# Loading w_in in four transfers of 128 partitions, with v read by even and odd columns

## The chip, the cores and the metric

The kernel runs on one core of a Trainium2 chip. The metric is the device time of one execution in microseconds (us). The core has a matrix engine (PE, whose weight loads are listed apart as PEld), a vector engine (DVE), a scalar engine (ACT), GpSimd (POOL) and a queue engine (SP); transfers run on 16 DMA engines.

## What is computed

Causal attention with 16 extra "beacon" keys in front that every query sees, and behind it a two-layer network with ELU between the layers. The heads of the attention, side by side, are the rows that the network takes.

```python
# q, k, v: (B=8, H=8, S=576, D=64); beacon_k, beacon_v: (8, 8, 16, 64)
k_all = np.concatenate([beacon_k, k], axis=2)
v_all = np.concatenate([beacon_v, v], axis=2)
scores = scale * np.matmul(q, k_all.transpose(0, 1, 3, 2))
scores = np.where(causal, -1000000000.0, scores)
a = softmax(scores)
x = np.matmul(a, v_all).transpose(0, 2, 1, 3).reshape(B * S, H * D)   # (4608, 512)
h = x @ w_in                                   # w_in (512, 2048)
g = np.where(h > 0.0, h, np.exp(np.minimum(h, 0.0)) - 1.0)
out = g @ w_out                                # w_out (2048, 512)
```

## The kernel before

Attention goes batch by batch (b = 0 to 7), the network by tiles of 512 tokens (tile 0 and 1 of 256 each, so that the network can begin early). The program is one list of steps in a string (from line 824 on). Each word names a step and its numbers, and the steps' instructions go to their engines in the order of that list; nothing reorders them. Each engine works through its own instructions in that order, and a wait of one instruction holds up all that stand behind it on its engine.

The steps that matter here:

- `lq.b.n.h0.h1` loads q and k of batch b (segment n, heads h0 to h1), `lv.b.j` a block j of 128 keys of v (with j = 0 also the beacon rows), `wi` a part of w_in, `wo.i` a quarter of w_out. All of these are transfers issued by POOL, which also turn fp32 into 16-bit numbers on the way. `s` and `J` store results through SP's queue.
- `T` transposes q and k on PE, `ck` and `cq` copy the result out of PSUM, `S` multiplies keys and queries, `x` takes the exponential on ACT, `m` masks on DVE.
- `L` sums the exponentials with a weight of ones on PE, `n` makes the reciprocal on ACT, `W` multiplies with v on PE, and `M` scales the product on DVE and writes it to xT, the network's input with features on the partitions. `W` and `L` use `quad` (line 381): four heads at a time, each in 32 columns of the PE array. A head has 64 columns of v, so it takes two such products, called halves. Half t of heads 4g to 4g+3 becomes chunk 2g + t of xT.
- `F.t.i` multiplies xT by two (tiles 0 and 1) or one (later tiles) column blocks of w_in, each over 4 chunks. `e`, `u`, `r`, `k`, `g` make the ELU, `G` and `Q` multiply with w_out.
- `wm` and `wh` multiply zeros on PE; their results aren't used.

w_in lies in SBUF as 128 partitions x 4 chunks x 2048 columns. The order of its rows follows from the halves: before, half t takes columns 32t to 32t+31 of a head, so partition 32i + d of chunk 2g + t is row 256g + 64i + 32t + d of w_in. One transfer, `wi.c.n` (line 158), brings 32 partitions (i) of two chunks (g) and one half of the columns (c): 32 x 2 pieces of 4 KB, 128 KB once in 16 bits. Sixteen of them load the whole. `F.0.0` to `F.0.3` and `F.1.0` to `F.1.3` use the lower half of the columns (c = 0), the next blocks the upper.

In the list two of the sixteen stand ahead of `lv.0.2`, the last block of v that `W.0.A` needs; six more of the lower half stand ahead of `F.0.1`, and the eight of the upper half between `lv.0.4` and `wo.0`.

Of the kernel before, what the change touches and what calls it, by code (L numbers as in the profile page):

```python
# [17 lines left out]
def kernel(  # L18
# [11 lines left out]
    nc = tc.nc  # L30
    P = 128

    B, H, S, D = q.shape
# [4 lines left out]
    DF = moe_w_in.shape[1]  # L38
# [7 lines left out]
    kc = [min(P, SK - P * j) for j in range(NKC)]  # L46
# [53 lines left out]
    w_in16 = konst.tile([P, NCC, DF], FP16, name="w_in16")  # L100
# [51 lines left out]
                nc.gpsimd.dma_start(  # L152
                    out=vt[b][0:NB, 0, :, :], in_=beacon_v[b].rearrange("h n d -> n h d"))

    wi_v = moe_w_in.rearrange("(g i t d) f -> i d g t f", i=4, t=2, d=32)
    wo_v = moe_w_out.rearrange("(f p) m -> p f m", p=P)

    def load_wi(c, n):
        f_ = slice(DF // 2 * c, DF // 2 * (c + 1))
        g, i = n // 4, n % 4  # L160
        nc.gpsimd.dma_start(
            out=w_in16[32 * i:32 * (i + 1), 2 * g:2 * g + 2, f_], in_=wi_v[i, :, g, :, f_])

    def load_wo(i):
        nc.gpsimd.dma_start(out=w_out16[:, 4 * i:4 * (i + 1), :], in_=wo_v[:, 4 * i:4 * (i + 1), :])
# [3 lines left out]
    for b in range(B):  # L169
        (nc.sync if b % 2 == 0 else nc.scalar).dma_start(  # L170
            out=bk32[NB * b:NB * (b + 1), :, :],
            in_=beacon_k[b].rearrange("h n d -> n h d"))
    zero = lo[:, 2 * DM:3 * DM].bitcast(BF16)
    nc.vector.memset(zero, 0.0)
    ones = konst.tile([P, 32], FP16)
# [81 lines left out]
        load_qk(b, n_, h0, h1)  # L257

    @step
    def wi(c, n):  # L260
        load_wi(c, n)

    @step
    def T(b, p, n_):
# [39 lines left out]
    def et(b, p):  # L304
        if (b, p // 2) not in ets:
            ets[b, p // 2] = attn.tile([P, 2, EC2], FP16, tag="et", bufs=3, name="et")
        return ets[b, p // 2][:, :, ECOLS * (p % 2):ECOLS * (p % 2 + 1)]
# [73 lines left out]
    def quad(b, g, qa, qe, t, half, first):  # L381


        v16 = None if half is None else vt[b]
        pcs = [(j, max(a, qa), min(e, qe), c + max(a, qa) - a) for (j, a, e, c) in lays[b]
               if max(a, qa) < min(e, qe)]
        for n, (j, a, e, c) in enumerate(pcs):
            for i in range(4):
                h, p = 4 * g + i, 2 * g + i // 2
                nc.tensor.matmul(  # L390
                    out=t[32 * i:32 * (i + 1), a - qa:e - qa],
                    lhsT=ones[0:kc[j], :] if half is None else v16[0:kc[j], j, h, 32 * half:32 * (half + 1)],
                    rhs=et(b, p)[0:kc[j], i % 2, c:c + e - a],
                    start=(first and n == 0), stop=(n == len(pcs) - 1), skip_group_check=True)

# [21 lines left out]
    @step  # L417
    def L(b, g):


        if g == "A":
            t = bank("ops", name="la")
            for i in range(2):
                quad(b, i, 0, CUT, t[:, CUT * i:CUT * (i + 1)], None, i == 0)
            lt[b, g] = t
        elif g == "B":
            t = psum.tile([P, 2, 512], FP32, tag="S", name="lt")
            for i in range(2):
                quad(b, i, CUT, S, t[:, i, 0:S - CUT], None, True)
            lt[b, g] = t[:, :, 0:S - CUT]  # L430
        else:
            t = hd[b, g] = psum.tile([P, 1024], FP32, tag="S", name="lt")
            r_ = lt[b, g] = t[:, 512 - QA:512 - QA + S]
            if (b, g) in presum:
                for i in range(4):
                    nc.tensor.matmul(  # L436
                        out=r_[32 * i:32 * (i + 1), QA:S], lhsT=ones,
                        rhs=presum[b, g][:, i // 2, i % 2, QA:S], start=True, stop=True, skip_group_check=True)
            else:
                quad(b, g, QA, S, r_[:, QA:S], None, True)  # L440
            quad(b, g, 0, QA, r_[:, 0:QA], None, True)
            for half in range(2):
                quad(b, g, 0, QA, t[:, 512 - QA * (3 - half):512 - QA * (2 - half)], half, True)
# [383 lines left out]
    S.0.0.3 S.0.0.1 cb.1.0 x.0.0.3 lq.0.0.4.8 T.0.2.0 cq.0.2.0 T.0.3.0 x.0.0.1 S.0.1.2 x.0.1.2 wm.5  # L827
    S.0.1.1 x.0.1.1 wm.5 S.0.1.3 x.0.1.3 tri m.0.0.3 m.0.0.0 lq.0.1.4.8 T.0.2.1 cq.0.3.0 S.0.0.2
    x.0.0.2 wm.5 S.0.3.0 T.0.3.1 x.0.3.0 cq.0.2.1 lq.1.0.0.4 S.0.2.0 x.0.2.0 wm.5 S.0.2.1 x.0.2.1
    lv.0.0 lv.0.1 wm.5 S.0.2.3 x.0.2.3 wi.0.0 wi.0.7 lv.0.2 wm.4 T.1.1.0 ck.1.1.0 T.1.0.0 m.0.2.0  # L830
    m.0.1.0 m.0.3.0 L.0.A n.0.A m.0.1.2 m.0.0.2 cq.0.3.1 S.0.3.1 x.0.3.1 cq.1.0.0 W.0.A.0 M.0.A.0
    S.0.3.3 S.0.2.2 x.0.3.3 x.0.2.2 W.0.A.1 m.0.2.3 m.0.3.3 m.0.1.3 M.0.A.1 wh.3 S.0.3.2 wh.5 S.1.2
    x.0.3.2 x.1.2 wh.4 S.1.5 wi.0.5 wi.0.1 x.1.5 wi.0.3 wi.0.6 wi.0.2 wi.0.4 F.0.1 e.0.1 cb.1.1
    S.1.3 x.1.3 F.0.0 u.0.0 e.0.0 lv.0.4 wi.1.0 m.0.3.2 r.0.1 cb.1.2 m.0.2.2 L.0.B lv.0.3 wi.1.3
    W.0.B.0 n.0.B M.0.B.0 g.0.1 S.1.4 F.0.2 x.1.4 S.1.1 e.0.2 x.1.1 k.0.0 W.0.B.1 M.0.B.1 lq.1.0.4.8
    T.1.2.0 ck.1.2.0 r.0.2 g.0.2 F.1.1 u.1.1 e.1.1 T.1.3.0 cq.1.3.0 S.1.6 wi.1.1 cb.1.3 x.1.6 wi.1.7
    wi.1.6 wi.1.5 wi.1.2 wi.1.4 F.0.4 S.1.0 m.1.0.1 wo.0 e.0.4 r.0.4 g.0.4 x.1.0 F.1.7 e.1.7 k.1.1
    r.1.7 g.1.7 S.1.12 x.1.12 S.1.7 cb.2.2 G.0.0.0 x.1.7 F.0.5 e.0.5 r.0.5 S.1.9 x.1.9 g.0.5 F.0.7
    e.0.7 r.0.7 S.1.10 x.1.10 S.1.11 x.1.11 G.0.1.0 F.0.3 g.0.7 m.1.0.0 D.1.0.0 u.0.3 S.1.8 x.1.8
    e.0.3 m.1.1.0 D.1.1.0 k.0.3 F.1.6 u.1.6 cb.2.1 e.1.6 lq.2.0.0.8 T.2.3.0 ck.2.3.0 T.2.2.0  # L840
# [134 lines left out]
```

## Time and profile before

| | |
|---|---|
| median of 3 runs | 331.85 us (331.82 to 331.98) |
| the profiled execution | 332.93 us, of which the span of the profile is 331.2 us |
| granted clock of PE, mean | 0.994 |
| w_in | 16 transfers of 128 KB, median 6.7 us from issue to landing |
| v | 24 of 128 KB, 8 of 112 KB, 8 of 80 KB and 8 of 16 KB (beacons) |
| transfers issued by POOL | 94912 packets, 18.49 MB |

The span begins with the first instruction that the profile shows and ends with the last; times in the traces are us from its start. "Idle before" is time in which an engine waited, with what released it. Sizes of transfers are those that land, in 16 bits; w_in and w_out are read as fp32, twice as much. A line of a view by stretches has the stretch, its length, then busy us and, in brackets, the number of instructions of PE, PEld, DVE, ACT and POOL, then the granted clock of PE (1.00 is full), the DMA share and GB/s landed.

### The profile page before, as it was taken

To read this page: it belongs to the slowest core of one execution; us is meant where nothing else is said; L and a number is where in the kernel's file an instruction comes from. 1 tells how busy PE (TensorE), PEld (TensorE's weight loads), DVE (VectorE), ACT (ScalarE), POOL (GpSimd) and SP (SyncE) were. 2 spreads that over 40 slices of the span, in tenths; PEclk is the share of its full clock that TensorE was granted. 3 is DMA by queue.
4 is the path that set the end of the run, shared out by engine and by line. 5 is a ranking of instruction groups with operands and counts; after the bars stand their busy time and mean duration, and the time that the engine had idled before them with its cause. 6 is when DMAs were issued, how large, how long until landed. Compare 5 with 4: busy or idle time off the path is not lost.

```text
span 331.2 us, 8770 instructions
## 1 busy us (share of the span) xinstructions
PE 321.2 (97%) x3572; PEld 213.8 (65%) x3572; DVE 300.4 (91%) x568; ACT 291.8 (88%) x481; POOL 100.7 (30%) x121
## 2 busy tenths in 40 slices
PE   8989999999999979999999999999999999999995
PEld 3545666544445546765676566756766888888884
DVE  3573999999999799999999999999999999999981
ACT  1989999799999979999999999999988778889941
POOL 8866745583049218900120348000000000000000
PEclk9998999999999999999999999999999999999999
DMA  9999999999989959999591995610111011020113
GB/s 115 141 165 186 204 196 174 163 154 175 65 90 133 147 138 87 193 170 165 75 148 53 119 71 109 91 35 2 63 36 34 0 65 64 2 97 33 34 65 127
DMA packets 129080, 34.65 MB, mean 105 GB/s; under 512 B 112912, under 2 KB 127504, under 8 KB 129040
## 3 DMA queue, kind: packets, MB, share of 16 engines
q0 software_dynamic: 94912, 18.49, 67.5%
q1 hardware_dynamic: 33552, 15.47, 21.3%
q8 instruction: 28, 0.46, 0.6%
q10 hardware_dynamic: 576, 0.13, 0.2%
q14 instruction: 12, 0.10, 0.1%
HBM read 37.22 MB, written 15.34 MB: 159 GB/s over the span
## 4 chain that ended last, share of the span: by engine, by line
PE 78%; DVE 7%; DMA 5%; ACT 4%; POOL 4%; SPq 1%; issue 1%; DVEq 0%; ACTq 0%; POOLq 0%
PE ops L650 25%; PE hps L528 20%; PE hps L732 11%; PE sc L330 6%; PE ut L390 5%; PE ops L575 4%; DMA v<-in_v_dram 3%; DMA out_dram<-osb 2%; PE ut L650 2%; DVE gt L553 1%; SPq L802 1%; DVE qk L410 1%; PE lt L436 1%; POOL qst L136 1%; POOL kst L136 1%
## 5 line engine op out<-in xcount | busy, mean ns | idle before, releaser
L345 ACT ACTIVATE et<-sc 128x1024 f16<-128x1024 f32 (+2 forms) x114 | 105.3, 988 | 3.3 <-PE sc L330 2.9
L528 PE MATMUL hps<-xT,w_in 128*128 128x512 f16 (+1 forms) x448 | 95.4, 350 | 1.7 <-ACT r L543 1.5
L650 PEld LDWEIGHTS <-gt 128*128 128x128 f16 x768 | 74.1, 98 | 16.3 <-issue 2.7
L528 PEld LDWEIGHTS <-w_in 128*128 128x128 f16 x448 | 40.9, 98 | 36.7 <-issue 6.2
L538 ACT ACTIVATE e<-hps 128x512 f32<-128x512 f32 x96 | 59.0, 626 | 3.2 <-DVE gt L553 2.0
L553 DVE SCALAR_TENSOR_TENSOR gt<-e,r 128x512 f16<-128x512 f32 x84 | 56.5, 681 | 0.0
L543 ACT ACTIVATE r<-hps 128x512 f16<-128x512 f32 x84 | 51.5, 622 | 3.1 <-PE hps L528 2.6
L147 POOL DMA_DIRECT2D v<-in_v_dram x40 | 44.1, 1192 | 26.4 <-PE ut L390 13.5
L650 PE MATMUL ops<-w_out,gt 128*128 128x256 f16 x368 | 48.4, 273 | 0.0
L650 PE MATMUL ops<-wt,gt 128*128 128x256 f16 x352 | 46.3, 273 | 0.2 <-DVE osb L671 0.2
L596 DVE TENSOR_TENSOR gt<-gt 128x1024 f16<-128x1024 f16 x48 | 32.3, 681 | 0.1
L771 DVE SCALAR_TENSOR_TENSOR gt<-e,r 128x512 f16<-128x512 f32 x48 | 31.8, 681 | 0.1
L350 DVE TENSOR_TENSOR et<-et,triu 128x1024 f16<-128x1024 f16 (+4 forms) x66 | 26.8, 447 | 2.5 <-ACT et L345 2.4
L742 ACT COPY kst<-hps 128x512 f32<-128x512 f32 x36 | 21.3, 594 | 5.6 <-PE hps L732 5.3
L390 PEld LDWEIGHTS <-v 128*32 128x32 f16 (+1 forms) x800 | 17.6, 96 | 12.0 <-issue 2.6
L390 PE MATMUL ut<-et,v 128*32 128x464 f16 (+3 forms) x560 | 21.1, 296 | 0.4 <-ACT et L345 0.4
L732 PEld LDWEIGHTS <-w_in 128*128 128x128 f16 x192 | 18.6, 98 | 2.9
L671 DVE TENSOR_TENSOR osb<-ops,sm 128x512 f32<-128x512 f32 x23 | 15.6, 683 | 3.6 <-DMA out_dram<-osb 2.3
L810 POOL MEMSET qst<- 128x96 bf16 x5 | 0.9, 178 | 55.8 <-PE sc L330 53.3
L410 DVE TENSOR_TENSOR qk<-qk,et 128x1344 f16<-128x1344 f16 (+2 forms) x30 | 17.5, 582 | 0.2
L488 DVE TENSOR_TENSOR xT<-ut,rl 128x672 f16<-128x672 f32 (+12 forms) x26 | 16.4, 668 | 0.2
L575 PE MATMUL ops<-w_out,gt 128*128 128x512 f16 x64 | 16.2, 381 | 0.0
(126 smaller groups left out, 524.6 us busy)
## 6 DMA issues: line engine op xcount, KB each, us to landing
out_dram<-osb SPq DMA_DIRECT2D x35, 256.0 KB, 2.3
v<-in_v_dram POOLq DMA_DIRECT2D x24, 128.0 KB, 8.1
scr<-in_q_dram POOLq DMA_DIRECT2D x5, 576.0 KB, 9.2
scr<-in_k_dram POOLq DMA_DIRECT2D x5, 576.0 KB, 13.9
w_in<-in_moe_w_in_dram POOLq DMA_DIRECT2D x16, 128.0 KB, 6.7
w_out<-in_moe_w_out_dram POOLq DMA_DIRECT2D x4, 512.0 KB, 10.8
v<-in_v_dram POOLq DMA_DIRECT2D x8, 112.0 KB, 6.2
v<-in_v_dram POOLq DMA_DIRECT2D x8, 80.0 KB, 5.8
```

The costliest lines, as they stand in the source:

```text
L147: nc.gpsimd.dma_start(out=vt[b][r0:r0 + n, j, :, :], in_=v[b, :, ilo[j]:ilo[j] + n, :].rearrange("h s d -> s h d"),)
L345: nc.scalar.activation(out=ets[b, d][:, :, a - EC2 * d:e - EC2 * d], in_=sc[b, g][:, :, a - c0:e - c0], func=AFT.Exp, bias=0.0, scale=SCALE)
L390: nc.tensor.matmul(out=t[32 * i:32 * (i + 1), a - qa:e - qa], lhsT=ones[0:kc[j], :] if half is None else v16[0:kc[j], j, h, 32 * half:32 * ...
L528: nc.tensor.matmul(out=h[:, n_, :], lhsT=w_in16[:, cc, P * fc:P * (fc + 1)], rhs=xt[k][:, cc, a - TT * k:e - TT * k], start=(cc == 0), sto ...
L538: nc.scalar.activation(out=eb[t, i], in_=flat(hp[t, i]), func=AFT.Exp, bias=0.0, scale=1.0)
L543: nc.scalar.activation(out=rb[t, i], in_=flat(hp[t, i]), func=AFT.Relu, bias=0.0, scale=1.0)
L553: nc.vector.scalar_tensor_tensor(out=half(t, i), in0=eb[t, i], scalar=1.0, in1=rb[t, i], op0=ALU.subtract, op1=ALU.min)
L575: nc.tensor.matmul(out=ob[t, tb_], lhsT=gt[:, fc, P * tb_:P * (tb_ + 1)], rhs=w_out16[:, fc, :], start=(fc == 0), stop=(fc == NFC - 1))
L596: (nc.vector if eng == "v" else nc.gpsimd).tensor_tensor(out=o_, in0=a_, in1=b_, op=op_)
L650: nc.tensor.matmul(out=xy[t, n_][qd], lhsT=lw[:, P * qd:P * (qd + 1)], rhs=wt_[:, c, :], start=(first and c == 0 and (qd == 0 or (t, n_) n ...
L732: nc.tensor.matmul(out=hx[t, g, n_][:, c, :], lhsT=lw, rhs=rh, start=(first and c == 0 and k_ == 0), stop=(k_ == 1), skip_group_check=True)
L771: eng.scalar_tensor_tensor(out=o_, in0=v_(eb[t, g, ph]), scalar=1.0, in1=v_(rb[t, g, ph]), op0=ALU.subtract, op1=ALU.min)
```

## The change

A half now takes every second column of a head: half t has columns t, t + 2, t + 4 and so on. So partition p of chunk 2g + t holds row 256g + 2p + t of w_in, the rows of one g are spread evenly over all partitions, and one transfer can bring 128 partitions x 2 chunks x half of the columns: four transfers in all, each with 128 x 2 pieces of 4 KB, 512 KB once landed. The weight that PE loads from v is read with a step of two elements. The steps `wi` have new numbers (first and last column block, g); the order of all other steps is the same.

```diff
-    wi_v = moe_w_in.rearrange("(g i t d) f -> i d g t f", i=4, t=2, d=32)
+    wi_v = moe_w_in.rearrange("(g p t) f -> p g t f", p=P, t=2)
 
-    def load_wi(c, n):
-        f_ = slice(DF // 2 * c, DF // 2 * (c + 1))
-        g, i = n // 4, n % 4
-        nc.gpsimd.dma_start(
-            out=w_in16[32 * i:32 * (i + 1), 2 * g:2 * g + 2, f_], in_=wi_v[i, :, g, :, f_])
+    def load_wi(f0, f1, g):
+        f_ = slice(P * f0, P * f1)
+        nc.gpsimd.dma_start(out=w_in16[:, 2 * g:2 * g + 2, f_], in_=wi_v[:, g, :, f_])
...
-                    lhsT=ones[0:kc[j], :] if half is None else v16[0:kc[j], j, h, 32 * half:32 * (half + 1)],
+                    lhsT=ones[0:kc[j], :] if half is None else v16[0:kc[j], j, h, half:D:2],
...
-    lv.0.0 lv.0.1 wm.5 S.0.2.3 x.0.2.3 wi.0.0 wi.0.7 lv.0.2 wm.4 T.1.1.0 ck.1.1.0 T.1.0.0 m.0.2.0
+    lv.0.0 lv.0.1 wm.5 S.0.2.3 x.0.2.3 wi.0.8.0 wi.0.8.1 lv.0.2 wm.4 T.1.1.0 ck.1.1.0 T.1.0.0 m.0.2.0
     m.0.1.0 m.0.3.0 L.0.A n.0.A m.0.1.2 m.0.0.2 cq.0.3.1 S.0.3.1 x.0.3.1 cq.1.0.0 W.0.A.0 M.0.A.0
     S.0.3.3 S.0.2.2 x.0.3.3 x.0.2.2 W.0.A.1 m.0.2.3 m.0.3.3 m.0.1.3 M.0.A.1 wh.3 S.0.3.2 wh.5 S.1.2
-    x.0.3.2 x.1.2 wh.4 S.1.5 wi.0.5 wi.0.1 x.1.5 wi.0.3 wi.0.6 wi.0.2 wi.0.4 F.0.1 e.0.1 cb.1.1
-    S.1.3 x.1.3 F.0.0 u.0.0 e.0.0 lv.0.4 wi.1.0 m.0.3.2 r.0.1 cb.1.2 m.0.2.2 L.0.B lv.0.3 wi.1.3
+    x.0.3.2 x.1.2 wh.4 S.1.5 x.1.5 F.0.1 e.0.1 cb.1.1
+    S.1.3 x.1.3 F.0.0 u.0.0 e.0.0 lv.0.4 wi.8.16.0 m.0.3.2 r.0.1 cb.1.2 m.0.2.2 L.0.B lv.0.3
     W.0.B.0 n.0.B M.0.B.0 g.0.1 S.1.4 F.0.2 x.1.4 S.1.1 e.0.2 x.1.1 k.0.0 W.0.B.1 M.0.B.1 lq.1.0.4.8
-    T.1.2.0 ck.1.2.0 r.0.2 g.0.2 F.1.1 u.1.1 e.1.1 T.1.3.0 cq.1.3.0 S.1.6 wi.1.1 cb.1.3 x.1.6 wi.1.7
-    wi.1.6 wi.1.5 wi.1.2 wi.1.4 F.0.4 S.1.0 m.1.0.1 wo.0 e.0.4 r.0.4 g.0.4 x.1.0 F.1.7 e.1.7 k.1.1
+    T.1.2.0 ck.1.2.0 r.0.2 g.0.2 F.1.1 u.1.1 e.1.1 T.1.3.0 cq.1.3.0 S.1.6 cb.1.3 x.1.6 wi.8.16.1 F.0.4 S.1.0 m.1.0.1 wo.0 e.0.4 r.0.4 g.0.4 x.1.0 F.1.7 e.1.7 k.1.1
```

More of the change, by code (lines that the diff above doesn't have):

```diff
@@ L259, in wi @@
     @step
-    def wi(c, n):
-        load_wi(c, n)
+    def wi(f0, f1, g):
+        load_wi(f0, f1, g)
     @step
```

## The prediction

> **What bounds the kernel now.** I read the engine shares first, then the busy time by stretches, then the chain that ended last, then the queue of the transfers in the one place where that chain leaves the engines.
>
> ```profile
> span 331.2 us, 8770 instructions
> PE 321.2 (97%) x3572; PEld 213.8 (65%) x3572; DVE 300.4 (91%) x568; ACT 291.8 (88%) x481; POOL 100.7 (30%) x121
> ...
> 20.00:27.00 7.00, 5.57 (x85) 2.52 (x85) 3.83 (x11) 5.73 (x8) 6.92 (x13) 0.76 1.23 154
> 27.00:40.00 13.00, 12.73 (x247) 8.82 (x245) 8.33 (x17) 11.95 (x18) 8.98 (x13) 1.00 1.26 202
> ...
> 60.00:80.00 20.00, 20.00 (x172) 8.92 (x169) 19.16 (x36) 18.23 (x29) 13.04 (x13) 1.00 2.04 165
> ```
>
> The stretches give, behind their length, the busy time of PE, weight loads, DVE, ACT and POOL, then the granted clock, the DMA share and GB/s. From 27 us on PE is never free for more than some tenths in a stretch, and it works through one fixed order. Time lost ahead of 27 us is therefore not made up later, unless a later wait with a date of its own swallows it. The stretch from 20 to 27 us is the weak one: 1.43 us without work and a granted clock of 0.76. The chain says why:
>
> ```profile
> 11.53 0.91 POOL v L147
> 12.44 1.03 POOL w_in L161 x2
> 13.47 8.61 DMA v<-in_v_dram
> ...
> 22.13 0.39 PE ua L390 x15
> ...
> 26.58 1.25 PE hps L528 x8
> ```
>
> POOL issues a v transfer, two of w_in, then the next v (step lv.0.2, the third 128 keys of batch 0). That v travels 8.61 us, and PE, in the midst of W.0.A.0, starts again within 0.1 us of its landing. Everything up to here is a chain of POOL issues and one queue; from here on it is PE.
>
> **The queue at that place.** The list of issues gives size and time to landing, POOL's timeline the starts:
>
> ```profile
> 12.42 1.09 POOL L161 DMA_DIRECT2D w_in<-in_moe_w_in_dram  x2
> 13.47 0.94 POOL L147 DMA_DIRECT2D v<-in_v_dram  x1
> 15.93 0.55 POOL L161 DMA_DIRECT2D w_in<-in_moe_w_in_dram  x1 [1.51 <-DMA qst<-in_q_dram]
> ...
> v<-in_v_dram POOLq DMA_DIRECT2D x1, 128.0 KB, 8.9
> w_in<-in_moe_w_in_dram POOLq DMA_DIRECT2D x1, 128.0 KB, 8.5
> ...
> w_in<-in_moe_w_in_dram POOLq DMA_DIRECT2D x1, 128.0 KB, 8.4
> v<-in_v_dram POOLq DMA_DIRECT2D x1, 128.0 KB, 8.6
> ```
>
> Adding: lv.0.1 (from 11.53) lands at 20.4, the two w_in (12.42 and 12.96) at 20.9 and 21.4, lv.0.2 at 22.1. They land in the order of their issue, each some half microsecond behind the one ahead of it. The third row shows the other rule of this queue: the 17th transfer waits for the 9th to land (8 in flight).
>
> **Part 1: two wide transfers ahead of lv.0.2.** The change takes away wi.0.0 and wi.0.7 (128 KB each, as landed in fp16) and puts wi.0.8.0 and wi.0.8.1 (128 partitions, 512 KB each) at the same place. Six more quarters thus come ahead of lv.0.2, which stood behind it before. I price a wide one three ways:
>
> ```profile
> 30.00:32.00 2.00, 2.00 (x64) 1.44 (x53) 0.13 (x1) 1.95 (x4) 0.92 (x2) 1.00 1.23 203
> ...
> 29.61 0.53 POOL L161 DMA_DIRECT2D w_in<-in_moe_w_in_dram  x1 [0.88 <-DMA w_in<-in_moe_w_in_dram]
> 31.11 0.78 POOL L165 DMA_DIRECT2D w_out<-in_moe_w_out_dram  x1 [0.96 <-DMA qst<-in_q_dram]
> ...
> w_in<-in_moe_w_in_dram POOLq DMA_DIRECT2D x1, 128.0 KB, 6.7
> ...
> w_out<-in_moe_w_out_dram POOLq DMA_DIRECT2D x1, 512.0 KB, 8.0
> ```
>
> - A queue filled with such weights moves 203 GB/s (30 to 32 us): 524,288 bytes take 2.6 us.
> - The nearest single transfer, w_out with 512 KB over 128 partitions, lands at 31.11 + 8.0 = 39.1, behind the last w_in at 29.61 + 6.7 = 36.3: 2.8 us, the upper bound.
> - Four narrow ones at the spacing of the pair above (0.97 us for two, so 0.48): 1.9 us, the lower bound.
>
> I take 2.6, because the rate is an average over many transfers, and a spacing of two short ones may lie within their overlap. Then lv.0.2 lands 2 x 2.6 - 0.97 = **4.2 us later** (2.9 to 4.6), at 26.3 in place of 22.1. POOL's longer issue (w_out took 0.78 us, so 0.5 us more for the pair) is covered by those seconds of queue; without that cover it would be the 0.5.
>
> What waits behind: on PE, in order, the rest of W.0.A.0, S.0.3.3, W.0.A.1, the fillers wh and S.1.2. For S.0.3.3 ACT waits, for W.0.A.0 DVE:
>
> ```profile
> 21.14 0.85 ACT L345 ACTIVATE et<-sc 128x832 f16<-128x832 f32 x1
> 22.85 2.38 ACT L345 ACTIVATE et<-sc 128x832 f16<-128x832 f32 x3 [0.86 <-PE sc L330]
> ...
> 22.66 0.69 DVE L498 TENSOR_TENSOR xT<-ua,rl 128x512 f16<-128x512 f32 x1 [1.62 <-PE ua L390]
> ```
>
> The idle time in front of each (in brackets) shows that both are already out of work in that gap, so neither can use the longer one to get ahead. All three shift together.
>
> **Part 2: the clock after the gap.**
>
> ```profile
> 22.13 0.39 PE L390 MATMUL ua<-et,v 128*32 128x16 f16 x16 [1.41 <-DMA v<-in_v_dram]
> ...
> 23.50:23.70 0.20, 0.20 (x1) 0.03 (x1) 0.20 (x2) 0.20 (x2) 0.20 (x1) 0.91 0.91 133
> 23.70:23.90 0.20, 0.18 (x3) 0.19 (x4) 0.16 (x2) 0.20 (x2) 0.20 (x1) 0.50 0.67 92
> ...
> 27.00:27.20 0.20, 0.20 (x3) 0.15 (x2) 0.00 (x0) 0.20 (x1) 0.20 (x1) 0.81 2.58 169
> ```
>
> PE's timeline has the gap (1.41 us ahead of 22.13, so from 20.7 on), and the stretches behind it the granted clock. The gap of 1.4 us is already followed by a half clock from 23.7 to 27.1. With a gap four times as long PE should start at half clock at once. If the dip then ends as long after the restart as now (5.0 us), it covers the first 1.6 us too, at most 1.6 us more; if it had ended before the restart, up to 1.7 us (half of 3.4) would come back. PE and ACT share this stretch, so a part is hidden; I take **+0.4** (-1.2 to +1.6). By the Trainium skill (TensorE: Matmul & The Clock Gate, "Part 1: The HAM clock gate") the gate judges fixed windows of about 3.4 us; the dip here is 3.4 us long, so the trace agrees. By that rule the half clock would run to about 30.5, which would add some 0.4 to 0.9 us.
>
> **Part 3: the rest of POOL's list.** Twelve issues fall away. Their 0.54 us each stand on POOL, which is no bound (30%). What is late next? With the prices above, behind lv.0.2 at 26.3 come lv.0.4, wi.8.16.0 (29.4), lv.0.3 (30.1), the second half of q and k of batch 1 (1.4 each, 32.9), wi.8.16.1 (35.5). The 1.4 is the time between the landings of that q and k now; their users stand below them:
>
> ```profile
> 24.46 0.69 POOL L136 DMA_DIRECT2D qst<-in_q_dram  x1
> 25.14 0.67 POOL L136 DMA_DIRECT2D kst<-in_k_dram  x1
> ...
> qst<-in_q_dram POOLq DMA_DIRECT2D x1, 288.0 KB, 6.4
> kst<-in_k_dram POOLq DMA_DIRECT2D x1, 288.0 KB, 7.1
> ...
> 30.14 1.25 PE L390 MATMUL ub<-et,v 128*32 128x320 f16 x40
> 34.32 0.45 PE L276 MATMUL tp<-identb,qst 96*64 96x96 bf16 x12
> 37.00 1.05 PE L528 MATMUL hps<-xT,w_in 128*128 128x256 f16 x8
> ```
>
> With the shift of 4.6 us W.0.B.0 (needs lv.0.3) comes at 34.7, T.1.2.0 (q, k) at 38.9, F.0.4 (upper half of w_in) at 41.6. Each has 4 us or more, so nothing new is waited for; the first F, at 26.5 before, did not wait for w_in, so having it early gains nothing. Cost 0; were the shift not there, W.0.B.0 alone would be close. Further on POOL's lv.2.1 waits for W.0.B.1 to free its buffer, which moves with PE; the queue has w_out, q and k of batch 2 to move in the meantime.
>
> **Part 4: every second column of v.** 800 weight loads read 32 columns two apart. No row of this trace has a weight read with a stride. Rows of contiguous loads, grouped:
>
> ```profile
> 10.35 0.30 PEld L330 LDWEIGHTS <-qk 64*128 64x128 bf16 x10 [0.59 <-DVE qk L289]
> 33.13 1.06 PEld L390 LDWEIGHTS <-v 128*32 128x32 f16 x40 [0.21 <-issue]
> 34.32 0.31 PEld L276 LDWEIGHTS <-qst 96*64 96x64 bf16 x12
> ...
> 57.78 1.50 PE ut L390 x40
> ```
>
> A load of 32 columns comes every 26.5 ns, of 64 every 26, of 128 every 30. A strided one spans 63 columns, so by the nearest row it costs nothing; by the farthest 3.5 ns x 800 = 2.8 us. A gain is excluded, since as many loads of as many columns remain. I take 0. The Trainium skill (SBUF — State Buffer, "Door 1: The DMA port swizzle") lets a stride of up to 8 two-byte elements go free; no run here shows it, and the sum stays.
>
> **Sum.** 4.2 + 0.4 + 0 + 0 = 4.6 us. The profiled execution took 332.93 us (its span 331.2 and 1.7 around it), so it would take 337.5. The median of the runs is 331.85, 1.1 lower; on that scale: **336.4 us**.
>
> **Rivals.**
> - *The wide transfer is cheap* (0.10). Between 20 and 27 us, with narrow transfers in flight, the queue moved 154 GB/s, and 202 after. If that is the narrow form and not POOL's issue pace, a wide one may go faster than any row here. Then four narrow ones at 0.48 us shrink by 154/202 to 1.5 us, lv.0.2 is late by 2 x 1.5 - 0.97 = 2.0, and the time is about 334. Against it: from 27 to 40 us narrow w_in and wide w_out share the 202. The skill's page SBUF — State Buffer, in the section named above, speaks for this case: 189 GB/s onto 32 partitions, 328 onto 128 at 1 MiB; an estimate by it is 1.6 us for a wide one, 334.1 in sum.
> - *Strided loads are slow* (0.08). If each takes twice as long, 40 loads take 2.1 us against the 1.50 of their matmuls: 0.6 more in each of 14 W steps, less than half of that in each of 14 L steps, about 1.5 in batch 0, some 12 us in all; with the shift, about 348. Against it: four columns of loads of different width cost the same above.
> - *lv.0.2 isn't held back* (0.07). Place: the queue between 20 and 26 us. Sixteen engines each serve their own share, and v's pieces could pass beside the weights. If lv.0.2 lands by 22.5, PE restarts as now and the twelve saved issues hide on POOL: 331.8, not slower. Against it: the four landings above, in order of issue. It decides from that landing alone: up to 22.7 the time is within 0.2%.
>
> **How the numbers follow.** The forecast has 0.75, with a range of its own of 334.7 to 338.5. The range for 8 in 10 goes down to 333.8 (most of the cheap transfer) and up to 339.5 (upper ends of transfer and clock, or a part of the stride's 2.8); below it lies the last rival, above it the slow loads. A measurement of this kernel tells 0.2% (0.7 us) from no change. Faster by more: 0.03 (the last rival, with a dip of the clock that goes away); within: 0.05; slower: 0.92.
>
> **What would show it.** Right: the chain again goes through lv.0.2, now with some 12.7 us in flight; PE's gap from 20.7 to about 26.3; half clock right after the restart; equal lengths afterwards, so that F.1.7, G.0.0.0 and all that follows lie 4 to 5 us later; the 40 loads of a W step still in about 1.06 us, and its matmuls in 1.50. Wrong: lv.0.2 landing before 24 (price of part 1), a new wait for q, k or w_in between 27 and 45 us (part 3), W steps over 1.6 us (part 4), or a shift at 45 us that is gone at 130 (that lost time stays lost).

## The result, and the profile after

| | before | after |
|---|---|---|
| median, first comparison | 331.92 us (4 runs) | 336.27 us (4 runs, 335.83 to 337.16), ratio 1.0118, interval 1.0091 to 1.0146 |
| median, second comparison | 332.41 us (29 runs) | 336.59 us (5 runs), ratio 1.0125, interval 1.0103 to 1.0147 |
| profiled execution | 332.93 us, span 331.2 | 336.41 us, span 334.7 |

The change costs 4.2 to 4.4 us by the medians, some 1.2%. The two profiled executions are only 3.5 us apart, because that of the kernel before is 1.1 us above its median. The page of the changed kernel has fewer instructions on POOL and nearly the same busy time on the other engines. The last row shown is the granted clock in 40 slices of 8.4 us:

```profile
span 334.7 us, 8748 instructions
PE 320.4 (96%) x3572; PEld 213.9 (64%) x3572; DVE 300.0 (90%) x568; ACT 291.5 (87%) x481; POOL 94.4 (28%) x109
...
PEclk9987999999999999999999999999999999999999
```

PE does the same work and the span is longer, so the time is a gap. The chain of waits shows where:

```profile
12.47 1.39 POOL w_in L160 x2
13.86 11.52 DMA v<-in_v_dram
25.38 0.04 issue
25.43 0.57 PE ua L388 x16
```

The same links as before, but lv.0.2 now travels 11.52 us. PE's timeline has the gap, the first F (the row of L526) and the first G (L573):

```profile
20.29 0.35 PE L388 MATMUL ua<-et,v 128*32 128x256 f16 x8
25.43 0.57 PE L388 MATMUL ua<-et,v 128*32 128x16 f16 x16 [4.78 <-DMA v<-in_v_dram]
...
29.95 1.05 PE L526 MATMUL hps<-xT,w_in 128*128 128x256 f16 x8
...
43.31 1.04 PE L573 MATMUL ops<-w_out,gt 128*128 128x512 f16 x4
```

In the profiled execution of before they began at 26.51 and 40.04:

```profile
26.51 1.31 PE L528 MATMUL hps<-xT,w_in 128*128 128x256 f16 x8
...
40.04 1.04 PE L575 MATMUL ops<-w_out,gt 128*128 128x512 f16 x4
```

Both are 3.3 to 3.4 us later now. The list of issues gives the landings behind that. The issues are at 11.55, 12.46, about 13.2 (half of the pair's 1.41 us behind its start) and 13.86:

```profile
w_in<-in_moe_w_in_dram POOLq DMA_DIRECT2D x1, 512.0 KB, 9.6
v<-in_v_dram POOLq DMA_DIRECT2D x1, 128.0 KB, 8.0
...
w_in<-in_moe_w_in_dram POOLq DMA_DIRECT2D x1, 512.0 KB, 11.4
v<-in_v_dram POOLq DMA_DIRECT2D x1, 128.0 KB, 11.5
```

lv.0.1 lands at 19.55, the wide pair at 22.1 and 24.6, lv.0.2 at 25.4: one wide transfer takes **2.5 us** of the queue. The stretches around the gap, with the granted clock behind the five engines:

```profile
21.00:22.00 1.00, 0.00 (x0) 0.00 (x0) 0.14 (x1) 1.00 (x2) 0.20 (x1) 0.96 1.20 203
22.00:23.00 1.00, 0.00 (x0) 0.00 (x0) 0.00 (x0) 0.08 (x1) 0.68 (x1) 0.50 1.76 181
...
28.00:29.00 1.00, 1.00 (x10) 0.30 (x10) 0.86 (x4) 0.55 (x2) 0.31 (x1) 0.63 1.37 199
29.00:30.00 1.00, 1.00 (x15) 0.42 (x15) 0.28 (x1) 1.00 (x2) 0.64 (x2) 1.00 1.29 207
```

The granted clock falls just before 22, in the midst of the gap. PE restarts at 25.43 at half clock and gets the whole back between 28 and 29.

### The profile page after: what moved, and what is told of

It reads as the page before. It is cut to its first block, busy times and chain, and to the rows that moved or that the text cites. A ratio compares the mean times of both kernels' runs of the same rounds, so it can differ in the third digit from the quotient of the medians.

```text
span 334.7 us, 8748 instructions
## 1 busy us (share of the span) xinstructions
PE 320.4 (96%) x3572; PEld 213.9 (64%) x3572; DVE 300.0 (90%) x568; ACT 291.5 (87%) x481; POOL 94.4 (28%) x109
## 4 chain that ended last, share of the span: by engine, by line
PE 76%; DVE 7%; DMA 6%; ACT 5%; POOL 4%; SPq 2%; issue 1%; DVEq 0%; ACTq 0%; POOLq 0%
PE ops L648 25%; PE hps L526 19%; PE hps L730 11%; PE sc L328 6%; PE ut L388 5%; PE ops L573 4%; DMA v<-in_v_dram 3%; DMA out_dram<-osb 2%; PE ut L648 2%; ACT et L343 2%; SPq L800 2%; DVE gt L551 1%; DVE qk L408 1%; PE lt L434 1%; POOL qst L136 1%
## 5 line engine op out<-in xcount | busy, mean ns | idle before, releaser
L526 PE MATMUL hps<-xT,w_in 128*128 128x512 f16 (+1 forms) x448 | 95.1, 349 | 1.8 <-ACT r L541 1.6
L526 PEld LDWEIGHTS <-w_in 128*128 128x128 f16 x448 | 40.8, 98 | 36.6 <-issue 6.0
L573 PE MATMUL ops<-w_out,gt 128*128 128x512 f16 x64 | 16.2, 381 | 0.0
```

Source lines behind the costliest of these rows:

```text
L526: nc.tensor.matmul(out=h[:, n_, :], lhsT=w_in16[:, cc, P * fc:P * (fc + 1)], rhs=xt[k][:, cc, a - TT * k:e - TT * k], start=(cc == 0), sto ...
L573: nc.tensor.matmul(out=ob[t, tb_], lhsT=gt[:, fc, P * tb_:P * (tb_ + 1)], rhs=w_out16[:, fc, :], start=(fc == 0), stop=(fc == NFC - 1))
```

## The experiments

Each ran beside the kernel before on one chip. The first four share 23 runs of it (median 332.37), the next four 29 (332.41), the last two 17 (332.19). The three groups are on three chips, so between groups the ratios to before are compared and not the times.

**1. lv.0.2 first, then the wide pair.**

```diff
-    ... wi.0.8.0 wi.0.8.1 lv.0.2 ...
+    ... lv.0.2 wi.0.8.0 wi.0.8.1 ...
```

> The changed kernel with lv.0.2 issued ahead of the two wide transfers; nothing else moves. Queue theory (lv.0.2 is late because two times 512 KB stand ahead of it): lv.0.2 lands at about 20.3 us, right behind lv.0.1 (19.6 in the changed kernel, plus 0.7), PE's gap of 4.8 us goes away, and the wide pair lands at about 22.8 and 25.3 us, ahead of the first F; the time falls by at least the gap, to 330 to 331.5 us, below the kernel before, which has a gap of 1.4 us itself. Rival (wide form or rest of POOL's list costs the time): it stays within 1 us of 336.3. Rival (strided weight loads cost it): it falls by the gap only if the W steps are not longer, and stays above 334 otherwise.

331.49 us, ratio to before 0.9982 (0.9967 to 0.9998). PE's timeline:

```profile
20.19 0.56 PE L388 MATMUL ua<-et,v 128*32 128x256 f16 x24
...
24.73 1.10 PE L526 MATMUL hps<-xT,w_in 128*128 128x256 f16 x8
...
28.15 1.53 PE L388 MATMUL ub<-et,v 128*32 128x320 f16 x40
```

All 24 products of W.0.A.0 run in one piece, with no wait, and F begins 5.2 us earlier than in the changed kernel. One word moved forward takes back the whole loss, with wide transfers and strided columns still there: it was the place of lv.0.2 in the queue. The last row points to a new wait: W.0.B.0 takes 1.53 us in place of 1.25, as lv.0.3 now comes late, behind wi.8.16.0 (lv.0.3 is issued at 18.63 and lands 10.2 us later, at 28.8).

**2. The columns alone.**

```diff
-    wi_v = moe_w_in.rearrange("(g i t d) f -> i d g t f", i=4, t=2, d=32)
+    wi_v = moe_w_in.rearrange("(g i d t) f -> i d g t f", i=4, t=2, d=32)
...
-                    ... v16[0:kc[j], j, h, 32 * half:32 * (half + 1)],
+                    ... v16[0:kc[j], j, h, half:D:2],
```

> The kernel before with even and odd columns of v alone: sixteen narrow transfers of w_in at their old places, each with the rows that the new halves need. Queue theory, with a stride that costs nothing: 331.9 us, within 0.3, and 40 loads of a W step still about 1.06 us. Rival (strided loads cost): up to 2.8 us more by the row of 128 columns, some 8 more if each load took twice as long; the whole change's 4.4 us would then show up here in part or in full.

331.85 us, ratio 0.9993 (0.9978 to 1.0009): no difference that shows. The weight loads' timeline has the row that answers to 1.06 us before:

```profile
28.79 1.09 PEld L390 LDWEIGHTS <-v 128*32 128x32 f16 x40
```

The chain of the same kernel has the matmuls of a W step at 1.51 us, against 1.50. A stride of two elements in the weights costs nothing here.

```profile
56.48 1.51 PE ut L390 x40
```

PE's timeline of this kernel showed something that I had not counted on. lv.0.2 landed early (at 20.9), and then the first F stops after two products:

```profile
20.90 0.39 PE L390 MATMUL ua<-et,v 128*32 128x16 f16 x16 [0.17 <-DMA v<-in_v_dram]
...
25.02 0.38 PE L528 MATMUL hps<-xT,w_in 128*128 128x256 f16 x2
25.69 0.82 PE L528 MATMUL hps<-xT,w_in 128*128 128x256 f16 x6 [0.30 <-DMA v<-in_v_dram]
```

F doesn't read v, so the name of the releaser can't be right; the last narrow transfer of w_in that this F needs landed at about 25.4. In experiment 1, with the same work of the other engines and w_in there earlier, this F runs through. Experiments 5 and 8 have the same stop.

**3. Eight narrow transfers ahead of lv.0.2.**

```diff
-    ... wi.0.0 wi.0.7 lv.0.2 ...
+    ... wi.0.0 wi.0.7 wi.0.5 wi.0.1 wi.0.3 wi.0.6 wi.0.2 wi.0.4 lv.0.2 ...
-    ... S.1.5 wi.0.5 wi.0.1 x.1.5 wi.0.3 wi.0.6 wi.0.2 wi.0.4 F.0.1 ...
+    ... S.1.5 x.1.5 F.0.1 ...
```

> The kernel before with all eight narrow transfers of the lower half of w_in ahead of lv.0.2; columns and width as before. Queue theory: as many bytes stand ahead of lv.0.2 as in the changed kernel. The eight issues take longer on POOL, with at most eight transfers in flight, so lv.0.2 is issued at about 21 us and lands at 25.5 to 26.5; the time is 335.5 to 337.5 us. Rival (the width of 128 partitions costs the time, not the place): lv.0.2 lands within 1 us of 22.1 and the time stays at 331.9 to 333.

337.69 us, ratio 1.0163 (1.0143 to 1.0183), even slower than the wide pair and 0.2 us above the range that was expected. PE's timeline:

```profile
25.55 0.56 PE L390 MATMUL ua<-et,v 128*32 128x16 f16 x16 [4.93 <-DMA v<-in_v_dram]
```

The same bytes in narrow form hold lv.0.2 back as long. Here it is POOL as well: with eight in flight it could issue lv.0.2 only at 20.06, and it lands 5.4 us after that.

**4. Fillers in front of W.0.A.0 in the changed kernel.** Their results aren't used.

```diff
-    ... cq.1.0.0 W.0.A.0 ...
+    ... cq.1.0.0 wh.80 W.0.A.0 ...
```

> The changed kernel with twenty products of zeros of 512 columns on PE (some 4.3 us) in front of W.0.A.0, so that PE is not idle while lv.0.2 travels. lv.0.2 lands as in the changed kernel, at 25.4 us. What it tells is the price of the half clock: if the clock stays at 1.00 and that term is the 0.4 us of the prediction (up to 1.6), the time is 0.2 to 1.6 us below the changed kernel's 336.3. Rival (the half clock is the greater part of the loss): 333.5 or less. Rival (the clock costs nothing because ACT sets the pace there): 336.3, unchanged.

334.95 us, ratio 1.0077 (1.0061 to 1.0094); granted clock 0.998 to 1.000 in every run. PE's timeline:

```profile
19.80 4.49 PE L221 MATMUL wh<-lo 128*128 128x512 bf16 x20
24.22 0.36 PE L388 MATMUL ua<-et,v 128*32 128x256 f16 x8
25.50 0.39 PE L388 MATMUL ua<-et,v 128*32 128x16 f16 x16 [0.92 <-DMA v<-in_v_dram]
...
28.98 1.05 PE L526 MATMUL hps<-xT,w_in 128*128 128x256 f16 x8
...
30.29 1.05 PE L526 MATMUL hps<-xT,w_in 128*128 128x256 f16 x8
```

lv.0.2 lands as late as in the changed kernel, and yet the loss shrinks. Against the changed kernel the ratios differ by 0.0048 (1.0125 less 1.0077), 1.6 us of 332.4: that is the price of the half clock, with a wide margin. The two ratios are from two sets of runs on two chips, and each has an interval of some 0.2% to either side, so the price lies between some 0.7 and 2.5 us. The profiles put it lower: from the restart of W.0.A.0 to the first G it takes 16.90 us here (25.50 to 42.40), 17.88 in the changed kernel (25.43 to 43.31) and 18.21 in its second profile (experiment 7), so 1.0 to 1.3 us more. Both rivals fall: the half clock is neither the greater part of the loss nor free.

**5. Fillers in the kernel before.** The same edit with wh.24.

> The kernel before with six products of zeros of 512 columns on PE (1.3 us) in front of W.0.A.0. Most executions of the kernel before had a granted clock of 0.998 to 1.0, a few 0.993 or 0.994 (the profiled one among them). If its gap costs a half clock only now and then, the fillers change the median by less than 0.5 us and take away the clocks of 0.994. Rival (the half clock is a steady part of the time before): 331.3 or less.

332.47 us, ratio 1.0009 (0.9991 to 1.0028): nothing, as expected, but the clocks of 0.994 did not go away. Two of twelve runs still had one, and the profiled one of them shows why for itself: its clock was at half from 123.8 to 127.2 us, behind another gap of PE (1.56 us ahead of 122.12, waiting for ACT). And its first F waits for w_in, so a quicker W.0.A doesn't help:

```profile
26.30 0.82 PE L528 MATMUL hps<-xT,w_in 128*128 128x256 f16 x6 [0.65 <-DMA v<-in_v_dram]
```

**6. One wide transfer ahead of lv.0.2.**

```diff
-    ... wi.0.8.0 wi.0.8.1 lv.0.2 ...
+    ... wi.0.8.0 lv.0.2 wi.0.8.1 ...
```

> The changed kernel with lv.0.2 issued between the two wide transfers: one time 512 KB stands ahead of it in place of two. Queue theory, 2.5 us for a wide one: lv.0.2 lands 2.5 us earlier than in the changed kernel, at about 22.9 us; PE's gap is about 2.2 us, so the half clock is mostly gone; the time is 331.9 to 334. Rival (a threshold, such as eight transfers in flight or the clock, and not the bytes): as slow as with two, 336, or as fast as with none, 331.5.

333.18 us, ratio 1.0019 (1.0003 to 1.0035): between none (ratio 0.9982) and two (1.0125). PE's timeline, and below it a stretch of the same kernel:

```profile
22.29 0.39 PE L388 MATMUL ua<-et,v 128*32 128x16 f16 x16 [1.58 <-DMA v<-in_v_dram]
```

```profile
24.00:25.00 1.00, 0.67 (x7) 0.20 (x9) 1.00 (x5) 1.00 (x2) 0.00 (x0) 0.51 1.45 206
```

The landing goes with the bytes ahead, 20.0, 22.3 and 25.4 to 25.5 us for none, one and two. Counted from the landing of lv.0.1 in the same execution, it comes 0.8, 3.3 and 5.8 us later: 2.5 us for each wide transfer. The half clock wasn't "mostly gone" as expected: 11 of 12 runs had 0.989 to 0.995; the gap was 1.6 us in the profiled one.

**7. The changed kernel again, and lv.0.2 and lv.0.3 first.** The second edit goes on from experiment 1.

```diff
-    ... lv.0.4 wi.8.16.0 m.0.3.2 r.0.1 cb.1.2 m.0.2.2 L.0.B lv.0.3
+    ... lv.0.4 lv.0.3 wi.8.16.0 m.0.3.2 r.0.1 cb.1.2 m.0.2.2 L.0.B
```

> The changed kernel once more, beside the others on one chip: 335.8 to 337.2 us, granted clock 0.99 in every execution, lv.0.2 landing between 25 and 26 us.

336.59 us, clock 0.988 to 0.990 in all five runs, lv.0.2 landing at 25.5:

```profile
25.56 0.57 PE L388 MATMUL ua<-et,v 128*32 128x16 f16 x16 [5.02 <-DMA v<-in_v_dram]
```

The first G begins at 43.77.

> The changed kernel with lv.0.2 ahead of the first wide pair and lv.0.3 ahead of the third wide transfer, as W.0.B.0 waited for lv.0.3 when only lv.0.2 was moved (its 40 products took 1.53 us in place of 1.25). Queue theory: lv.0.3 lands by 26.5 us, W.0.B.0 takes 1.25 us again and no later step waits for a transfer; the time is 0.3 to 0.7 us below that of the kernel with lv.0.2 alone moved (331.5), 330.8 to 331.2. Rival (the engines behind, not the queue, set the pace there): 331.5, unchanged.

331.37 us, ratio to before 0.9968 (0.9951 to 0.9984): the lowest time of all, 1.0 us under the kernel before, but above the range that was expected. PE's timeline:

```profile
24.83 1.05 PE L526 MATMUL hps<-xT,w_in 128*128 128x256 f16 x8
...
28.20 1.25 PE L388 MATMUL ub<-et,v 128*32 128x320 f16 x40
```

W.0.B.0 takes 1.25 us again. Whether that gains anything over experiment 1 the times do not tell: the two ratios' intervals overlap, and in the profiled executions the first G starts at 38.2 in both.

**8. Narrow transfers with lv.0.2 first, and the kernel before again.**

```diff
-    ... wi.0.0 wi.0.7 lv.0.2 ...
+    ... lv.0.2 wi.0.0 wi.0.7 ...
```

> The kernel before with lv.0.2 ahead of the two narrow transfers; all sixteen stay narrow. lv.0.2 lands near 20 us, as with the wide ones behind it. Theory (the narrow form holds the first F up by its issue: with eight in flight and 0.54 us each, the last of the lower half lands at 25.4 to 26.3 us, as in the run with the columns alone and in the one with fillers before): F.0.1 still waits for w_in until then, and the time stays at 331.8 to 332.4, some 0.5 to 1 us above the wide kernel with v first. Rival (v's place is all, the width of the transfers brings nothing): as fast as that kernel, 331.4, with F.0.1 at 24.8.

332.90 us, ratio 1.0013 (0.9993 to 1.0032), 0.5 us above the range that was expected. Moving lv.0.2 alone gains nothing as long as w_in is narrow:

```profile
25.50 0.38 PE L528 MATMUL hps<-xT,w_in 128*128 128x256 f16 x2 [0.31 <-PE sc L330]
26.50 0.81 PE L528 MATMUL hps<-xT,w_in 128*128 128x256 f16 x6 [0.62 <-DMA w_in<-in_moe_w_in_dram]
```

Now the wait has the name that it should have. In this execution even the moved lv.0.2 landed late, at 21.6; what stood ahead of it in the queue was slow (lv.0.1 landed at 20.3). Its first G stood another 0.49 us for w_out, which is issued behind all the narrow transfers:

```profile
40.53 1.02 PE L575 MATMUL ops<-w_out,gt 128*128 128x512 f16 x4 [0.49 <-DMA w_out<-in_moe_w_out_dram]
```

> The kernel before once more, for a second profile: lv.0.2 lands between 20.8 and 22.1 us, and unless the clock is halved again the first F waits for w_in until 25.5 to 26.3 us; 331.3 to 333.2 us.

331.88 us. In PE's timeline of this second execution of the kernel before, lv.0.2 lands at 21.4, F comes at 25.41, and the clock stays at 1.00:

```profile
21.43 0.39 PE L390 MATMUL ua<-et,v 128*32 128x16 f16 x16 [1.01 <-DMA v<-in_v_dram]
...
25.41 1.23 PE L528 MATMUL hps<-xT,w_in 128*128 128x256 f16 x8 [0.44 <-PE sc L330]
...
26.90 1.05 PE L528 MATMUL hps<-xT,w_in 128*128 128x256 f16 x8
```

The first F starts 0.44 us late and takes 1.23 us in place of 1.05. The last two narrow transfers that it needs land at about 25.1 and 25.6, so it is w_in that it waits for here, though the row names S on PE.

## Why the prediction was right, point by point

**The place and the mechanism: right.** The wait behind lv.0.2 grew, as forecast, and experiments 1 and 6, which move one step each, and 3, which moves six narrow transfers, show that the bytes ahead of it in the queue set it. The forecast was 336.4, the measurement 336.27. That they are so close is in part luck. The prediction added its terms to the one profiled execution, which gave 337.5; the profiled execution after took 336.41. So from profile to profile the forecast was 4.6 us and the measurement 3.5. Going over to the median took 1.1 us off, and that made up for it: the profiled execution of before was a late one. Its first G came 1.2 us later than in the second profile (40.04 and 38.87), 0.7 us because lv.0.2 landed later and the rest behind that, where its clock dipped and that of the second did not. By the sign that the prediction gave, F and G 4 to 5 us later, it also missed against its own profile (3.3 to 3.4 us); against the second profile of before the first G is 4.4 us later. The ends of the range are rougher than the sum: the lowest and the highest terms give 331.85 + 2.9 - 1.2 = 333.6 and 331.85 + 4.6 + 1.6 = 338.1, where the prediction says 334.7 and 338.5.

**That lost time stays lost: right, and the best tested of all steps.** The table has the start of the first G and the span for each profiled execution:

| kernel | first G, us | span, us | difference |
|---|---|---|---|
| before; again | 40.04; 38.87 | 331.2; 330.2 | 291.2; 291.3 |
| changed; again | 43.31; 43.77 | 334.7; 335.2 | 291.4; 291.4 |
| lv.0.2 first; lv.0.2 and lv.0.3 first | 38.20; 38.23 | 329.6; 329.6 | 291.4; 291.4 |
| columns alone; narrow, lv.0.2 first | 38.74; 40.53 | 329.9; 331.9 | 291.2; 291.4 |
| eight narrow ahead; one wide ahead | 44.15; 40.28 | 335.6; 331.5 | 291.5; 291.2 |
| changed, with fillers | 42.40 | 333.8 | 291.4 |
| before, with fillers | 40.42 | 332.9 | 292.5 |

From the first G on eleven of twelve need 291.2 to 291.5 us, whatever went on ahead; the last lost one more around 124 to 127 us, as told above. The differences of time are decided in the first 44 us.

**The price of a wide transfer: right.** Forecast 2.6 us (1.9 to 2.8), measured 2.5 twice. In the profile of before, six narrow transfers behind lv.0.2 landed 0.65 us apart, from 22.7 to 25.9, so four of them also take 2.6; the 0.48 of the lower bound was too short. The row of stretches was the better guide than the spacing of two short ones.

**The delay of lv.0.2: 4.2 forecast; it depends on what one compares with.** Against the one execution that the prediction had, it is 3.3 us (22.1 to 25.4); against the second one 4.0 (21.4 to 25.4). The part of the queue ahead of all this varies: lv.0.1, which the edits leave alone up to its issue, landed at 20.4 in the first profile and at about 18.9 in the second. Counted from the landing of lv.0.1, which leaves that out, lv.0.2 came 1.7 and 2.5 us later in the two profiles of before and 5.8 in both of the changed kernel. So the pair holds it back by 3.3 to 4.2 us, and the 4.2 of the forecast is the upper end.

**The half clock: there, as forecast, but its size holds for one base only.** Forecast +0.4, with 1.6 at most. Against the profiled execution of before, which has a dip itself, it is less: from the restart of W.0.A.0 to the first G it takes 17.91 us before (22.13 to 40.04), 17.88 and 18.21 in the two profiles of the changed kernel. Against a full clock it is 1.0 to 1.3 us by the profiles and 1.6 by the medians (experiment 4). And the full clock is the base of the median: of the 69 runs of the kernel before in the three sets, 60 had a granted clock of 0.998 or more; the profiled one, at 0.994, was among the few. So for most runs the dip is new. It started as forecast, ahead of the restart. But its end isn't tied to the restart, as the prediction assumed with its 5.0 us: it came 3.3 us behind the restart in one profile of the changed kernel and 4.1 in the other. By stretches of half a microsecond, the clock is at half for 6.8 us in both (21.9 to 28.7 and 22.8 to 29.7), and for 3.4 in the profile of before (23.7 to 27.1). By the Trainium skill (TensorE: Matmul & The Clock Gate, "Part 1: The HAM clock gate") the clock is judged in windows of 3.4 us; dips of one and of two such lengths fit that.

**"Having w_in early gains nothing": wrong.** This is the sentence of part 3 that failed. In the one execution that the prediction had, F was late through the half clock, and no wait for w_in showed. In experiments 2, 5 and 8, where W.0.A came earlier, F stood 0.3 to 0.65 us for the last narrow transfer that it needs, and in the second profile of before it started 0.44 us late. From the restart of W.0.A.0 to the second F it takes 5.47 us in the second profile of before (21.43 to 26.90) and 4.79 with the wide pair and a full clock (25.50 to 30.29 in experiment 4): 0.7 us that the early w_in gives back, of which 0.5 are left at the first G (17.44 us from the restart against 16.90). With that one execution at a clock of 1.00 as the base, the terms up to the first G are 4.00 for the later restart, -0.54 for the early w_in and +0.98 for the half clock. They add up to the 4.44 us by which G is later (38.87 to 43.31), and the medians say 4.2 to 4.4. Two terms of the forecast, the half clock and the early w_in, were too small in opposite ways on this base, and its total was right partly for that reason. What part 3 said of W.0.B.0 held: without the shift it is close, and in experiment 1 it waits for lv.0.3.

**The stride: right.** Forecast 0, and experiment 2 shows no difference, to within some 0.7 us; the rival with slow loads (348 us) falls. What the prediction held against that rival, rows of contiguous loads of three widths, told nothing of a stride; the experiment does.

**The other rivals fall too.** The wide transfer isn't cheap (2.5 us, not 1.5), so the estimate from the Trainium skill's page SBUF — State Buffer, "Door 1: The DMA port swizzle", 1.6 us, doesn't hold at this place; a wide transfer took as long as four narrow ones in a full queue (2.5 us against 4 x 0.65). And lv.0.2 didn't pass the weights: it landed behind both wide transfers (24.6 and 25.4 us).

## What to carry to other kernels

Merging small transfers into large ones moves bytes forward, and here they landed in the order of issue: before merging, look for the small transfer behind them that somebody waits for, and put it first. Here the merge with v in front was worth some 0.6 to 1.0 us by the medians (experiments 1 and 7; experiment 7 moved lv.0.3 too), against nothing that shows for v in front of narrow ones, and with v behind it cost about 5 against that. And an engine that one profiled execution shows at half clock may run at full clock in most others: compare the clocks of all runs before taking a dip as part of the base.

## What the runs showed of the hardware

The delay of the queue isn't the same from run to run of one kernel: lv.0.2 landed at 22.1 and at 21.4 us in two executions of the kernel before, and lv.0.1 ahead of it at 20.4 and 18.9. The granted clock of PE was 0.988 to 0.990 in all nine runs of the changed kernel (gaps of 4.8 and 5.0 us in the two profiled) and 0.989 to 0.995 in 11 of 12 runs with one wide transfer ahead (1.6 us in the profiled one). In the profiled executions of narrow w_in it fell behind a gap of 1.4 us in W.0.A.0, and not behind gaps of 0.17, 0.79 and 1.01 us; twenty products of zeros kept it at 0.998 or more. In the profile of the changed kernel it fell 1.3 us into the gap, which began at 20.6. The Trainium skill (TensorE: Matmul & The Clock Gate, "HAM oscillation — how this bites in real kernels") names idle gaps of more than about 3.4 us as the danger; here 1.4 to 1.6 us among short products was enough.
